# The second chunk's strided heads on TensorE in pairs, and a new order for the first chunk's heads

## The chip, the cores and the metric

One core of a Trainium2 chip runs the kernel. The metric is device time in microseconds (us), from one launch; the time given for a kernel is the median of several runs. The core's engines are named as the profile names them: PE (TensorE matmuls; PEld its weight loads), DVE (VectorE), ACT (ScalarE), POOL (GpSimd) and SP (SyncE, which here issues nearly all DMAs). Every engine carries out its own instructions strictly in the order in which they stand in its queue.

## What is computed

Attention with two kinds of masks, and then a two-layer network on its output:

```python
scores = scale * np.matmul(q, k.transpose(0, 1, 3, 2))        # 8 batches, 8 heads, 576 rows, 64 wide
mask_local = (rel >= 0) & (rel < 32)                           # heads 0 to 3
mask_strided = (rel >= 0) & (pos[None, :] % 32 == pos[:, None] % 32)   # heads 4 to 7
attn = softmax(where(mask, scores, -1e9))
x = (attn @ v) as 4608 x 512
h = np.maximum(x @ w_in, 0.0)                                  # 512 -> 2048
out = h * h @ w_out                                            # 2048 -> 512
```

All of it is in 32-bit floats. For the network the kernel splits each operand into a high and a low part and adds three products (high by high, low by high, high by low), so that one step of a layer costs three matmuls.

## The kernel before, in words

The 4608 tokens are worked off in 12 chunks of 384. For each chunk the attention of its rows comes first and fills four tiles of x: `xlh`, `xll` (local heads, high and low part) and `xsh`, `xsl` (strided heads). Then the network runs in 16 steps. `up` (L452) makes one 128-row slice of h from the four tiles: 12 matmuls of 384 columns (L462), the first 6 from the local tiles and the last 6 from the strided ones. ACT and DVE square it and split it (L470 to L476). `down` (L480) follows two steps later and adds 9 matmuls of 512 columns into three accumulators (L489). So PE has 21 matmuls in each of 16 x 12 steps, and the attention of chunk c+1 has to be finished while the network of chunk c runs.

Attention is done in three ways:

- **Pairs on PE** (`pe_pair`, L292): two heads at a time, from a tile `qk` that holds both heads' 64 rows. Five steps: load; scores on PE (L319) and row minima with the mask on DVE (L324); softmax (POOL subtracts the minima, L347, ACT takes the exponential, L348, DVE sums, L349, and takes the reciprocal, POOL multiplies, L353); transposes on PE (L359) and their copies from PSUM (L360); products with v on PE (L367 local, L378 strided), and the high and low part of x (ACT L382, DVE L383). In the first chunk both the local pairs (`first`) and the strided pairs (`late`) go this way, ahead of everything else. In the second chunk only the local pairs do (`local(c)`), and they have one PSUM bank, number 3, for all that PE writes: each write waits until the bank has been read out. The first chunk's local pairs use a shorter form, `single`, in which ACT subtracts the minimum, takes the exponential and sums in one instruction for each window (L345).
- **Strided heads on POOL and DVE** (`strided`, L386): products on POOL and sums on DVE, row by row: q by k (L412, L413), softmax (L418 to L425), attention by v (L434, L435), and transposes (L441). Chunks 2 to 12 of the 12 do their strided heads so.
- **Local heads one at a time on PE** (`pe_head`), from the third chunk on: among others the parts `kx` and `qx` (L217 to L220) and scores (L234).

While the first chunk's network runs, the weights are still arriving. `convert` (L147) turns each of 16 loads into a high and a low part, in two cuts of 512 columns: ACT scales the load (L154), makes `z` (L166) and the high part (L172), DVE joins two halves (L169), POOL makes the low part (L173). Two cuts belong to each step of the network (`WRATE`).

What sets the order: the main loop (L631) hands out the work by step. `SPREAD` (L43) says over how many steps of the running chunk the next chunk's local and strided work is handed out, here 11 and 8 in the first chunk. The program is then scheduled at build time, engine by engine, from the framework's own forecast of the time; the order in the finished queues is therefore not the order of the code. `zeros` (L583) are products of zeros on PE during the opening: 60, and then twice 30.

Of the kernel before, what the change touches and what calls it, by code (L numbers as in the profile page):

```python
# [17 lines left out]
HL = H // 2  # L18
# [24 lines left out]
SPREAD = ((11, 8), (13, 13))  # L43
# [43 lines left out]
def attn_moe(ctx: ExitStack, tc, qk_l, v_l, qk_d, v_d, qk_p, v_p, f_s, q_s, k_s, v_s, w_in, w_out, masks, eye, out):  # L87
# [59 lines left out]
    def convert():  # L147
# [9 lines left out]
        for k in range(NFT):  # L157
# [4 lines left out]
            for raw, at in cuts:  # L162
# [13 lines left out]

                if not at and k + 1 < NFT and k + 1 in raws:
                    with tc.issue_after(first_step.ins):
                        scale(k + 1)
# [112 lines left out]
    def pe_pair(c, pr, local, qk, vr, es, pt, banks, sm, single):  # L292
# [3 lines left out]
        if local:  # L296
            kw, wins, nv = KW, [at for _, _, at in windows(c)], P
            src, vsrc = qk_d[c, pr], v_d[c, pr]
            mk = [mask_sb[:QC, w % 2, :] for w in range(NW)]
        else:  # L300
            kw, wins, nv = QC, [QC * w for w in range(NW)], QC
            src, vsrc = qk_p[pr], v_p[pr]
            mk = [mask_sb[:QC, 3, :QC]] * NW
# [12 lines left out]
        e4 = [e[:QC, : NW * kw].rearrange("p (w k) -> p w k", k=kw) for e in es]  # L316
# [25 lines left out]
        for h in range(2):  # L342
            if single:
                for w in range(NW):
                    last["a"] = nc.scalar.activation(e4[h][:, w], e4[h][:, w], AF.Exp, bias=nm[:QC, h, w : w + 1], scale=-1.0, accum_out=ss[:QC, NW * h + w, :1])  # L345
# [6 lines left out]
        for h in range(2):  # L352
            last["g"] = nc.gpsimd.tensor_mul(e4[h], e4[h], rs[:QC, h].unsqueeze(2).broadcast_to([QC, NW, kw]))  # L353
        yield
        p4 = pt.rearrange("p (h w q) -> p h w q", h=2, w=NW)
        for h in range(2):
# [3 lines left out]
            last["a"] = nc.scalar.copy(pt[:kw, h * TC : (h + 1) * TC], t[:kw, :TC])  # L360
        yield
        x = x_tiles(c)
        if local:
# [4 lines left out]
            outs = [(o[:, :TC], [x["l", s][:, pr, :] for s in "hl"])]  # L368
        else:

            r0 = D * pr
            outs = []
            for a in range(2):
                o = s_ps[a]
# [5 lines left out]
                outs.append((o[r0 : r0 + D, :TC].rearrange("p (s r i) -> p s i r", s=2, i=SI), [by_i(x["s", s][:, a, :]) for s in "hl"]))  # L380
        for src, (xh, xl) in outs:
            last["a"] = nc.scalar.copy(xh, src)  # L382
            last["v"] = nc.vector.tensor_sub(xl, src, f32(xh))  # L383
# [156 lines left out]
    def local(c):  # L540
        heads = [pair_at(c, pr, True, pr, "3") for pr in range(2)]
        for h in (0, 0, 1, 0, 1, 0, 0, 1, 1, 1):
            next(heads[h])
            yield
# [58 lines left out]
    with tc.issue_after(last["p"].ins):  # L603
        zeros(0, NWARM // 2)
        for k in range(NEARLY, 8):
            fetch(k)
    next(late[0])
    with tc.issue_after(last["p"].ins):
        zeros(1, NWARM // 2)
    next(first[0])  # L610
    next(first[1])
    weights = behind({"a": last["a"]}, ungated)
    next(late[1])
    for i in range(2):
        next(first[0])
        next(first[1])
        next(late[0])
        next(late[1])
        if i:
            weights = behind({"a": last["a"]}, ungated)  # L620
        for _ in range(2):
            next(weights)
    next(late[0])
    next(late[1])
    for _ in range(2 * NEARLY - 4):
        next(weights)
# [4 lines left out]
    for s in range(NS + 2):  # L631
# [29 lines left out]
        if c + 1 < NCHUNK and s >= LATER:  # L661
            j0 = LATER if c == 0 else 0
            if j == j0:
                lo, st = local(c + 1) if c == 0 else iter(()), strided(c + 1)
                if c == 0:
                    lo, st = behind(heads_end, lo), behind(heads_end, st)
# [5 lines left out]
            while dl < fl * 10 and next(lo, "end") != "end":  # L672
# [14 lines left out]
def _layout(q, k, v, moe_w_in, moe_w_out):  # L687
# [22 lines left out]
    by_r = lambda t: rows(t[:, HL:], 0).reshape(HL, 2, SI, STR, D).transpose(0, 1, 3, 2, 4).reshape(HL, TC, D)  # L710
    a["qk_p"] = asc(np.concatenate([by_r(t).transpose(0, 2, 1) for t in (q, k)], axis=2)).reshape(2, P, 2 * TC)
    a["v_p"] = two(by_r(v).reshape(HL, NW, QC, D).transpose(0, 2, 1, 3).reshape(1, HL, QC, NW * D)).reshape(2, QC, 2 * NW * D)
# [45 lines left out]
```

## Time and profile before

| | us |
|---|---|
| median of 3 runs (883.71 to 884.16) | 883.96 |
| the profiled execution: its own time | 883.18 |
| its span, first to last instruction | 881.4 |
| first matmul of the network (L462) | 30.44 |
| first matmul of `down` (L489) | 39.17 |
| first matmul of the second chunk's network | 105.14 |

The 1.8 us between the profiled execution's own time and its span lie outside the instructions. The view of the timeline gives for each instruction its start and its duration; durations on one engine overlap a little, so starts, not durations, add up to the time. A bracket at the end of a row is idle time of the engine before it and what ended that. Matmuls with 32-bit operands appear as two records each.

### The profile page before, as it was taken

The page shows a single profiled execution, that of the slowest core. Times are in us where ns is not written, and L with a number is a line of the kernel's source. Part 1 is how long each engine was busy: PE and PEld are TensorE (multiplying, and loading weights), DVE is VectorE, ACT ScalarE, POOL GpSimd, SP SyncE. Part 2 cuts the span into 40 slices and gives each one's busy share as a digit, 9 for nine tenths or more (in the row PEclk, how much of TensorE's full clock was granted, in tenths as well). Part 3 has the DMA queues.
Part 4 walks back from the last instruction along what each step waited for, and adds up shares of the span by engine and source line. Part 5 has one row for each costly group of instructions (what it writes and reads, how often), then busy time and mean ns, then how long its engine had stood idle before and what let it go on. Part 6 is the DMA issues. An engine that isn't in the chain of part 4 may idle for free.

```text
span 881.4 us, 14862 instructions
## 1 busy us (share of the span) xinstructions
PE 868.5 (99%) x4744; PEld 789.6 (90%) x4744; DVE 635.5 (72%) x1892; ACT 572.6 (65%) x1510; POOL 676.8 (77%) x722
## 2 busy tenths in 40 slices
PE   8899999999999999999999999999999999999997
PEld 7788899999999999999999999999999989998996
DVE  4578687788777888878778778778787787883111
ACT  6798776676676666757657747657666665664332
POOL 4698878878978989898988978997898899782000
PEclk9999999999999999999999999999999999999999
DMA  9851631323123123104102302312131121000000
GB/s 356 355 195 63 184 121 42 103 84 113 32 66 112 37 89 103 44 30 127 44 13 80 115 14 74 104 31 74 31 102 57 30 71 61 7 1 10 28 1 36
DMA packets 26798, 71.41 MB, mean 81 GB/s; under 512 B 2976, under 2 KB 8736, under 8 KB 25184
## 3 DMA queue, kind: packets, MB, share of 16 engines
q1 hardware_dynamic: 26432, 70.14, 23.9%
q8 instruction: 37, 0.61, 0.3%
q10 hardware_dynamic: 288, 0.33, 0.1%
q14 instruction: 41, 0.34, 0.1%
HBM read 61.01 MB, written 9.44 MB: 80 GB/s over the span
## 4 chain that ended last, share of the span: by engine, by line
PE 95%; ACT 3%; DVE 1%; POOL 0%; issue 0%; DVEq 0%; POOLq 0%; ACTq 0%
PE h L462 44%; PE y L489 44%; PE s L234 2%; PE o L280 2%; ACT e L345 1%; PE w_ps L586 1%; ACT raw L154 1%; PE b L319 1%; DVE sc L419 0%; ACT z L166 0%; ACT w L172 0%; DVE raw L169 0%; ACT pt L360 0%; PE b L359 0%; DVE xsl L383 0%
## 5 line engine op out<-in xcount | busy, mean ns | idle before, releaser
L489 PE MATMUL y<-w,gh 128*128 128x512 f32 x1152 | 357.1, 391 | 0.8 <-ACT gh L475 0.8
L489 PEld LDWEIGHTS y<-w,gh 128*128 128x128 f32 x1152 | 212.5, 188 | 41.5 <-ACT gh L475 1.4
L462 PE MATMUL h<-xlh,w 128*128 128x384 f32 x768 | 229.6, 339 | 2.1 <-DVE xsl L383 1.6
L462 PE MATMUL h<-xsh,w 128*128 128x384 f32 x768 | 226.2, 335 | 0.0
L489 PE MATMUL y<-w,gl 128*128 128x512 f32 x576 | 224.0, 392 | 0.0
L434 POOL TENSOR_TENSOR pp<-vs,sc 128x448 f32<-128x448 f32 (+10 forms) x192 | 189.8, 1014 | 39.8 <-DVE qs L435 18.2
L412 POOL TENSOR_TENSOR pq<-ks,qs 128x512 f32<-128x512 f32 (+2 forms) x192 | 197.8, 1050 | 17.9 <-DVE sc L413 13.8
L476 DVE TENSOR_TENSOR gl<-h,gh 128x384 fp32r<-128x384 f32 x192 | 105.4, 550 | 84.2 <-ACT gh L475 82.9
L475 ACT CAST gh<-h 128x384 fp32r<-128x384 f32 x192 | 91.4, 477 | 103.0 <-PE y L489 100.0
L473 ACT ACTIVATE h<-h 128x384 f32<-128x384 f32 x176 | 83.0, 472 | 107.8 <-PE h L462 106.2
L413 DVE TENSOR_REDUCE sc<-pq 128x8 f32<-128x512 f32 (+4 forms) x228 | 119.6, 534 | 46.2 <-POOL pq L412 43.9
L462 PEld LDWEIGHTS h<-xlh,w 128*128 128x128 f32 x768 | 142.1, 188 | 5.6 <-DVE xsl L383 1.8
L462 PEld LDWEIGHTS h<-xsh,w 128*128 128x128 f32 x768 | 141.7, 188 | 0.3
L462 PE MATMUL h<-xll,w 128*128 128x384 f32 x384 | 129.3, 337 | 0.0
L435 DVE TENSOR_REDUCE qs<-pp 128x64 f32<-128x448 f32 (+11 forms) x192 | 106.7, 563 | 31.0 <-POOL pp L434 29.5
L489 PEld LDWEIGHTS y<-w,gl 128*128 128x128 f32 x576 | 108.1, 188 | 22.9
L462 PE MATMUL h<-xsl,w 128*128 128x384 f32 x384 | 128.5, 335 | 0.0
L474 ACT ACTIVATE h<-h 128x384 f32<-128x384 f32 x176 | 83.2, 473 | 3.6
L259 DVE STREAM_TRANSPOSE p_t<-e 32x128 f32<-32x128 f32 x240 | 72.3, 301 | 10.4 <-ACT e L248 6.0
L462 PEld LDWEIGHTS h<-xll,w 128*128 128x128 f32 x384 | 72.5, 189 | 2.2
L462 PEld LDWEIGHTS h<-xsl,w 128*128 128x128 f32 x384 | 72.2, 188 | 0.0
L243 ACT ACTIVATE e<-e,nm 96x128 f32<-96x128 f32 x160 | 62.5, 392 | 10.5 <-DVE nm L226 8.8
(97 smaller groups left out, 1077.2 us busy)
## 6 DMA issues: line engine op xcount, KB each, us to landing
qk<-qk_l SPq DMA_DIRECT2D x24, 400.0 KB, 3.2
y<-ysb SPq DMA_DIRECT2D x36, 256.0 KB, 3.7
raw<-w_in SPq DMA_DIRECT2D x7, 1024.0 KB, 11.2
qk<-qk_l SPq DMA_DIRECT2D x16, 416.0 KB, 3.3
vs<-v_s SPq DMA_DIRECT2D x10, 576.0 KB, 4.0
raw<-w_out SPq DMA_DIRECT2D x5, 1024.0 KB, 12.9
v<-v_l SPq DMA_DIRECT2D x40, 128.0 KB, 2.0
ks<-k_s SPq DMA_DIRECT2D x8, 576.0 KB, 3.8
```

What stands on the lines that cost most here:

```text
L243: nc.scalar.activation(e[:QC, cut(w)], e[:QC, cut(w)], AF.Exp, bias=nmax[:QC, w : w + 1], scale=-1.0, accum_out=ssum[:QC, w, :1])
L259: nc.vector.transpose(out=pt[STR * k : STR * (k + 1), :, STR * r : STR * (r + 1)], in_=e.rearrange("p (w k) -> p w k", k=KW)[STR * r : STR ...
L412: nc.gpsimd.tensor_mul(pv, kt[:, a : a + m, :], qt[:, i - i0 : i - i0 + 1, :].broadcast_to([P, m, D]))
L413: nc.vector.tensor_reduce(out=sc[:, i - i0, a : a + m], in_=pv, op=ALU.add, axis=AX.X)
L434: nc.gpsimd.tensor_mul(pv, vt[:, a : a + nd, :n], sc[:, il : il + 1, :n].broadcast_to([P, nd, n]))
L435: nc.vector.tensor_reduce(out=ot[:, il, a : a + nd], in_=pv, op=ALU.add, axis=AX.X)
L462: done = nc.tensor.matmul(ph[:, :TC], w[:, wsl], xx, start=n == 0, stop=n == 11)
L473: nc.scalar.activation(g, g, AF.Relu)
L474: nc.scalar.activation(g, g, AF.Square)
L475: last["gh"] = nc.scalar.copy(gh, g)
L476: nc.vector.tensor_sub(gl, g, f32(gh))
L489: done = nc.tensor.matmul(y_ps[c][t], g[:, sl], w[:, wsl], start=j == 0 and k == 0, stop=j == NFT - 1 and k == 2)
```

## The change

1. `local(c)` becomes `pairs(c)`: in the second chunk the strided pairs follow the local pairs, with the same buffers and the same single PSUM bank. `strided` is not run for that chunk; the host lays out `qk_p` and `v_p` for both chunks. The 20 steps are handed out over 12 network steps, the local pairs first.
2. Where a pair has one bank, its products with v take a bank for each half and are read out at once (`parts`), where before they were read out at the end.
3. In the first chunk the local pairs' exponentials are written to PSUM (`r4`) and multiplied from there by DVE instead of POOL, and the copies of the strided pairs' transposes (L360 before, L367 now) go from ACT to DVE.
4. The opening's steps come in a new order; the zeros are 60 and 20. The conversion of the first load's second cut is finished at once.

```diff
-SPREAD = ((11, 8), (13, 13))
+SPREAD = ((12, 8), (13, 13))
...
+                if k == 0 and at:
+                    split()
+                    split = None
...
+        r4 = [blocks(t) for t in s_ps] if single else e4
...
-                    last["a"] = nc.scalar.activation(e4[h][:, w], e4[h][:, w], AF.Exp, ...
+                    last["a"] = nc.scalar.activation(r4[h][:, w], e4[h][:, w], AF.Exp, ...
...
-            last["g"] = nc.gpsimd.tensor_mul(e4[h], e4[h], rs[:QC, h].unsqueeze(2).broadcast_to([QC, NW, kw]))
+            eng, key = (nc.vector, "v") if single else (nc.gpsimd, "g")
+            last[key] = eng.tensor_mul(e4[h], r4[h], rs[:QC, h].unsqueeze(2).broadcast_to([QC, NW, kw]))
...
-            last["a"] = nc.scalar.copy(pt[:kw, h * TC : (h + 1) * TC], t[:kw, :TC])
+            (nc.vector.tensor_copy if c == 0 and not local else nc.scalar.copy)(pt[:kw, h * TC : (h + 1) * TC], t[:kw, :TC])
...
+        def parts(src, dst):
+            last["a"] = nc.scalar.copy(dst[0], src)
+            last["v"] = nc.vector.tensor_sub(dst[1], src, f32(dst[0]))
...
-                o = s_ps[a]
+                o = s_ps[a] if s_ps else banks()
...
-    def local(c):
-        heads = [pair_at(c, pr, True, pr, "3") for pr in range(2)]
-        for h in (0, 0, 1, 0, 1, 0, 0, 1, 1, 1):
-            next(heads[h])
-            yield
+    def pairs(c):
+        for kind in (True, False):
+            heads = [pair_at(c, pr, kind, pr, "3") for pr in range(2)]
+            for h in (0, 0, 1, 0, 1, 0, 0, 1, 1, 1):
+                next(heads[h])
+                yield
...
-                lo, st = local(c + 1) if c == 0 else iter(()), strided(c + 1)
+                lo, st = (behind(heads_end, pairs(c + 1)), iter(())) if c == 0 else (iter(()), strided(c + 1))
...
-            while dl < fl * 10 and next(lo, "end") != "end":
+            while dl < fl * 20 and next(lo, "end") != "end":
```

What this does to the queues is seen in the finished order. Line numbers change: scores L319 become L325, transposes L359 L366, products with v L367 and L378 become L379 and L389, `up` L462 L470, `down` L489 L497, the low part of x L383 L373, POOL's subtraction and multiplication L347 and L353 become L353 and L360, its products L412 and L434 become L420 and L442.

First ACT's queue in the opening, where the last high parts of the strided heads' x (`xsh`) are made. Before:

```order
L382 CAST xlh_423<-b_1_1_218 128x384
L360 COPY pt_0_0_103<-b_0_0_280 96x384
L360 COPY w_1_0_104<-b_1_0_354 96x384
L382 CAST xsh_425<-b_0_0_279 64x384
L360 COPY w_1_0_104<-b_1_0_355 96x384
L166 ACTIVATE z_0_468<-raw_192 128x512
L172 CAST w_0_413<-raw_190 128x512
L154 ACTIVATE raw_194<-raw_194 128x1024
L382 CAST xsh_425<-b_0_0_280 64x384
L382 CAST xsh_425<-b_1_0_354 64x384
```

And now, at the same place of ACT's queue:

```order
L367 COPY pt_1_1_116<-b_1_1_218 128x384
L367 COPY pt_1_1_116<-b_1_1_219 128x384
L172 CAST w_0_372<-raw_190 128x512
L372 CAST xlh_384<-b_1_1_218 128x384
L372 CAST xsh_386<-b_0_0_248 64x384
L372 CAST xsh_386<-b_0_0_249 64x384
L372 CAST xsh_386<-b_1_0_313 64x384
L372 CAST xsh_386<-b_1_0_314 64x384
L166 ACTIVATE z_0_469<-raw_192 128x512
L154 ACTIVATE raw_194<-raw_194 128x1024
```

The four casts have moved ahead of the work on the second and third load, and the copies of the strided pairs' transposes have left the queue.

Next PE's queue at the border between the first and the second chunk's network; `b` is the pairs' PSUM bank, `h` the second chunk's first slices, `xlh` and `xll` its local x. Before, the last products of the pairs (`b`) lie among the first chunk's own steps, and the second chunk begins without any of them:

```order
L367 MATMUL b_1_1_1282<-pt_1_1_689,v_1_1_686 64x96 x8
L462 MATMUL h_14_1323<-xsh_425,w_7_1160 128x384 x2
...
L489 MATMUL y_2_614<-w_6_1218,gl_13_1307 128x512
L462 MATMUL h_0_1397<-xlh_901,w_0_413 128x384
L462 MATMUL h_0_1397<-xll_902,w_0_413 128x384
L462 MATMUL h_0_1397<-xlh_901,w_0_413 128x384 x2
```

Now the last local pair's products come after the second chunk's first six matmuls, and the whole of the strided pairs after that:

```order
L379 MATMUL b_1_1_969<-pt_1_1_648,v_1_1_645 64x96 x8
L470 MATMUL h_0_1392<-xlh_843,w_0_372 128x384
L325 MATMUL b_0_0_1039<-qk_0_0_1025 96x96 x4
L470 MATMUL h_0_1392<-xll_844,w_0_372 128x384
L325 MATMUL b_0_0_1048<-qk_0_0_1025 96x96 x4
L325 MATMUL b_1_0_1153<-qk_1_0_1030 96x96 x4
...
L366 MATMUL b_0_0_1210<-ident,e_0_0_1027 96x96 x4
L389 MATMUL b_0_0_1222<-pt_0_0_1029,v_0_0_1026 32x96 x8
...
L389 MATMUL b_1_0_1351<-pt_1_0_1034,v_1_0_1031 32x96 x8
L470 MATMUL h_0_1392<-xsl_846,w_0_372 128x384
...
L497 MATMUL y_0_571<-w_7_1199,gh_14_1309 128x512 x2
```

The strided pairs' scores, transposes and products stand in a row, with next to no matmul of the network between them, ahead of the second chunk's remaining matmuls and of the first chunk's last two `down` steps.

Last POOL's queue at the same place. `e` are the strided pairs' exponentials, `pp` and `pq` the products of `strided` for the third chunk, `kx` and `qx` parts of the third chunk's first local head:

```order
L353 TENSOR_TENSOR e_0_0_1028<-e_0_0_1028,nm_0_0_1037 96x384
L442 TENSOR_TENSOR pp_4_2_0_1626<-qkvs_4_1487,sc_4_1489 128x192
...
L353 TENSOR_TENSOR e_1_0_1032<-e_1_0_1032,nm_1_0_1151 96x384
...
L221 TENSOR_TENSOR kx_0_1335<-qk_0_1324,kx_0_1335 128x448
...
L360 TENSOR_TENSOR e_0_0_1027<-e_0_0_1027,rs_0_0_1038 96x384
...
L420 TENSOR_TENSOR pq_6_7_0_1751<-ks_6_1647,qs_6_1646 128x512
...
L360 TENSOR_TENSOR e_1_0_1032<-e_1_0_1032,rs_1_0_1152 96x384
...
L420 TENSOR_TENSOR pq_6_11_8_1844<-ks_6_1647,qs_6_1646 128x256
```

The second chunk's strided softmax shares POOL with the third chunk's strided heads, and the two alternate. DVE's queue interleaves them in the same way: between the four low parts of x (L373) stand the sums (L421) of the `pq` products.

53 lines of the change are left out of this document (25 added, 28 removed).

## Prediction

> **What bounds the kernel now.** I read the page first, then the timeline of PE for every stretch in which it stands idle, then the chain of waits for the opening.
>
> ```profile
> PE 868.5 (99%) x4744; PEld 789.6 (90%) x4744; DVE 635.5 (72%) x1892; ACT 572.6 (65%) x1510; POOL 676.8 (77%) x722
> ```
>
> PE is busy for all but 13 us. From the timeline of PE, the start of the first chunk's network, its first `down`, the one later gap, and the border to the second chunk:
>
> ```profile
> 30.44 0.69 PE L462 MATMUL h<-xlh,w 128*128 128x384 f32 x1 [1.61 <-DVE xsl L383]
> ...
> 39.17 1.66 PE L489 MATMUL y<-w,gh 128*128 128x512 f32 x6 [0.79 <-ACT gh L475]
> ...
> 89.56 0.44 PE L462 MATMUL h<-xlh,w 128*128 128x384 f32 x1 [0.48 <-DVE gl L476]
> ...
> 105.14 0.33 PE L462 MATMUL h<-xlh,w 128*128 128x384 f32 x1
> ```
>
> After 39.17 PE waits for another engine once, for 0.48. So work that leaves POOL and DVE is worth at most that 0.48, matmuls that are added to PE cost their full time, and time is to be had only ahead of 39.17. The stages of the opening, with the granted clock in the third column from the end:
>
> ```profile
> 25.00:30.00 5.00, 3.56 (x67) 2.85 (x66) 1.40 (x3) 4.13 (x8) 1.51 (x2) 1.00 1.01 422
> 30.00:35.00 5.00, 4.56 (x18) 4.56 (x19) 2.80 (x5) 4.69 (x9) 2.64 (x2) 0.66 1.01 405
> ```
>
> After a stretch with PE busy for 3.56 of 5 us, the clock falls for the network's first matmuls (0.66 on average), so the 36 `up` matmuls up to 39.17 take 8.7 us instead of the 6.3 that three times this row gives:
>
> ```profile
> 41.51 2.10 PE h L462 x12
> ```
>
> **The opening.** The network begins when the strided heads' low parts of x are made, and ACT's casts for them stand at the end of its queue. The chain of waits has the opening's prices on ACT:
>
> ```profile
> 8.76 6.27 ACT e L345 x32
> 15.03 1.08 ACT raw L154
> 16.11 0.41 ACT e L348
> 16.52 0.36 ACT pt L360
> ...
> 18.08 0.53 ACT z L166
> ...
> 19.72 0.36 ACT xlh L382
> ...
> 21.39 0.56 ACT w L172
> ...
> 30.42 0.87 DVE xsl L383 x2
> ```
>
> In the new order ACT has ahead of the last cast: the 16 window exponentials (6.27), 4 strided ones (1.7), 4 copies (1.5), 2 scalings (2.2), 2 `z` (1.1), 2 high parts (1.1) and 6 casts (2.2), together 16.1 us; from 8.76 that ends at 24.9. DVE now becomes the longer one:
>
> ```profile
> 0.00:30.40 30.40, 23.53 (x312) 20.48 (x312) 13.71 (x83) 20.75 (x60) 14.19 (x24) 1.00 0.95 372
> ```
>
> To its 13.7 us come four multiplications of 512 columns from PSUM (about 0.7 each, an estimate from the 0.55 that DVE takes for 384, below) and four copies (about 0.5), and one joining of weights comes later (0.6): 18 us. DVE starts just ahead of ACT's 8.76, so it ends at 26.5. The first matmul needs the bank that the second of the four low parts frees, some 0.7 before the end: 25.8. The 36 `up` matmuls take 6.3, the low clock about 1.8: the first `down` at 34.0 instead of 39.17, a gain of 5.2. Bounds: 2.6, if DVE keeps half of its old idle time, and 8, if ACT's sum is the limit and the clock stays up. The 40 zeros that go were hidden behind waits for the softmax; what they may cost is the clock of the opening's small matmuls, which is in the lower bound. That ACT now waits for the first two slices before it goes on with the weights belongs to the second rival.
>
> The removed POOL and DVE work of `strided` gives the 0.48, no more.
>
> **The added matmuls, if they were spread out.** Scores of one strided head, eight records one head after the other; transposes; products with v:
>
> ```profile
> 15.31 0.92 PE L319 MATMUL b<-qk 64*96 64x96 f32 x8
> ...
> 24.48 0.54 PE L359 MATMUL b<-ident,w 96*96 96x96 f32 x4 [1.34 <-POOL w L353]
> ...
> 27.32 1.51 PE L378 MATMUL b<-w,v 96*32 96x96 f32 x30 [0.28 <-ACT w L360]
> ```
>
> Without the last record's drain (a quarter of a microsecond) that is 0.68 a head for scores, 0.33 a head for transposes and 0.7 for each half of a pair's products: 4 x 0.68 + 4 x 0.33 + 4 x 0.7 = 6.8 us. Both heads of a pair alternately, as the first chunk issues them, cost less, here in the wider local form:
>
> ```profile
> 7.21 1.99 PE L319 MATMUL b<-qk 64*96 64x128 f32 x32
> ```
>
> That is 0.06 a record, against 1.04 us for eight (0.13) for one head at a time:
>
> ```profile
> 54.35 1.04 PE b L319 x8
> ```
>
> The second chunk's pairs don't do what the change's words say: in PE's queue they go one head at a time, so I take 0.68. The Trainium skill, TensorEngine Tiling (Array Packing), Tiling Modes, says that different tiles can load weights and multiply in parallel; by that rule, issued alternately, the scores would cost half and the sum would be 1.4 lower. The trace agrees with it in the first chunk.
>
> **Where they stand.** The queue decides more than the 6.8. At the border PE comes to the strided pairs with all other matmuls behind them: six of the second chunk's first 24 `up` matmuls are done, 18 and `down` 14 and 15 come later. So PE waits out the pairs' whole softmax, one bank at a time. POOL's share of that chain, from the groups by line and shape:
>
> ```profile
> L353 POOL TENSOR_TENSOR e<-e,rs 96x384 f32<-96x384 f32 x2 | 1.6, 822 | 0.0
> L347 POOL TENSOR_TENSOR e<-e,nm 96x384 f32<-96x384 f32 x2 | 1.6, 820 | 0.0
> L434 POOL TENSOR_TENSOR pp<-qkvs,sc 128x384 f32<-128x384 f32 x4 | 3.9, 964 | 0.0
> L434 POOL TENSOR_TENSOR pp<-qkvs,sc 128x320 f32<-128x320 f32 x4 | 3.5, 884 | 0.1
> L434 POOL TENSOR_TENSOR pp<-qkvs,sc 128x256 f32<-128x256 f32 x4 | 3.3, 816 | 0.0
> L434 POOL TENSOR_TENSOR pp<-qkvs,sc 128x192 f32<-128x192 f32 x4 | 2.2, 552 | 0.0
> L218 POOL TENSOR_TENSOR kx<-qk,kx 128x448 fp32r<-128x448 f32 x6 | 6.9, 1158 | 5.3 <-ACT kx L217 4.3 <-POOL xll L288 1.0
> L220 POOL TENSOR_TENSOR qx<-qk,qx 64x384 fp32r<-64x384 f32 x5 | 5.1, 1013 | 0.4
> L412 POOL TENSOR_TENSOR pq<-ks,qs 128x512 f32<-128x512 f32 x8 | 10.3, 1294 | 0.6 <-DVE qkvs L435 0.4 <-DVE sc L413 0.2
> L412 POOL TENSOR_TENSOR pq<-ks,qs 128x448 f32<-128x448 f32 x2 | 2.3, 1152 | 0.1
> L446 POOL TENSOR_TENSOR xsl<-qkvs,xsh 128x384 fp32r<-128x384 f32 x4 | 4.1, 1015 | 0.0
> L255 POOL TENSOR_TENSOR vx<-v,vx 128x256 fp32r<-128x256 f32 x5 | 3.7, 743 | 0.1
> ```
>
> And the hops on DVE and ACT:
>
> ```profile
> L324 DVE CUSTOM_DVE_ANT_0 e<-b,mask_sb 96x96 f32<-96x96 f32 x8 | 1.5, 243 | 0.0
> L349 DVE TENSOR_REDUCE sums<-e 96x4 f32<-96x384 f32 x2 | 1.1, 545 | 1.1 <-ACT e L348 1.1
> L383 DVE TENSOR_TENSOR xsl<-b,xsh 64x384 fp32r<-64x384 f32 x4 | 2.1, 553 | 3.8 <-ACT xsh L382 3.8
> L360 ACT COPY pt<-b 96x384 f32<-96x384 f32 x2 | 0.9, 475 | 0.0
> L382 ACT CAST xsh<-b 64x384 fp32r<-64x384 f32 x4 | 1.8, 472 | 0.3 <-PE b L378 0.3
> ```
>
> I count from the end of the last local pair's products. Cast and low part 1.0; scores 0.9; minima 1.0 (4 x 0.243); the second head the same 1.9: at 4.8 POOL can subtract its minima. From there POOL always has work, and its queue up to the last `pq` that DVE sums ahead of the last low part of x is: 3 subtractions (2.5), `pp` of 192, 256, 320 and 384 columns (3.2), `kx` and `qx` (2.2), 4 multiplications (3.3), `pq` of 448 and five of 512 (7.6), `xsl` and `vx` (1.8), and four short `pq` and a memset (about 2.3, an estimate from the sizes). Together 22.9. Then the sum of that `pq` (0.4), the low part (0.55), the last four `up` matmuls (0.9). End at 29.5. DVE sums each `pq` ahead of the low part that frees the bank, so the products with v and the second pair's transposes wait for POOL too; ACT's exponentials of the second pair stand behind a cast of `kx`, whose load cannot start before the strided scores free its buffer, but that ends ahead of POOL.
>
> The 18 `up` matmuls in this stretch would have cost 3.1 anyway. The stretch costs 26.4, the added matmuls included.
>
> **The clock.** With PE mostly idle for that long, the row at 30 us says that the clock falls; then the eight transposes and products after it take 4 us more, of which half lies behind POOL, and the next matmuls some 0.5: 2.5 in all. Both ends stay: 0 and 5.7 (4 and half of one 3.4 us stretch at half clock). The Trainium skill, TensorE: Matmul & The Clock Gate, Part 1, wants a whole idle window of about 3.4 us for the fall; by that rule alone a busier stretch stays at full speed and the sum is 2.5 lower. The trace shows the fall after a stretch that was mostly busy, so I go by the trace.
>
> **Sum**, against the profiled execution's own 883.2 (0.8 under the median): 883.2 - 5.2 - 0.5 + 26.4 + 2.5 = 906.4 us.
>
> **Rivals.** Two of them go by this row, a stretch of the first chunk's network (busy time of PE, PEld, DVE, ACT, POOL):
>
> ```profile
> 39.20:60.00 20.80, 20.80 (x107) 18.56 (x107) 16.88 (x46) 20.34 (x37) 18.04 (x19) 1.00 0.38 129
> ```
>
> *The queue behind the softmax is thinner.* If the third chunk's POOL work has been done before PE gets there, only the chain remains: 4.8 as above, the softmax's subtraction, exponential, sum, reciprocal and multiplication (0.8 + 0.5 + 0.5 + 0.4 + 0.8), for each pair two transposes with their copies (2.0) and two products with v, casts and low parts (3.9), and the last 0.9: 20.5 us, less 3.1. Then 883.2 - 5.7 + 17.4 = 895. For it: POOL was busy for 18.0 of 20.8 us, so it has some time in hand. Against it: POOL's new queue has that work after the strided subtractions, and a queue doesn't run ahead. 10%.
>
> *ACT becomes the bound of the first chunk.* Its work in a network step is two cuts and a slice, and it was busy for 20.3 of the 20.8 us. PE now starts 5 us earlier and asks for the weights earlier. If ACT follows only at its own pace, PE waits up to 5 us around the sixth slice: 911. For it: that share. Against it: ACT's opening ends as much earlier as PE's. 10%.
>
> *Faster.* The opening gains more than the border costs. It decides in this direction if the stretch at the border takes under 8.8 us, the opening's 5.2, the 0.5 and the 3.1: PE would have to find other matmuls while the pairs wait. With all of the wait filled and the opening's upper bound it is 883.2 - 8 - 0.5 + 6.8 = 881.5. For it: nothing but the short opening. Against it: a queue can't pass a waiting matmul, and the opening can't pay for the border by itself: the first load is scaled at 15.03, which with `z` and the high part is 2.2 on ACT, and joining and the low part on DVE and POOL are about as much again, so the network can hardly start before 20, which with the 2.4 of the slow first matmuls and the 0.5 is 13.3, under the 17.4 of the shortest chain. 3%, and 1% for no change.
>
> **How the numbers follow.** The forecast has 76%. The range runs from 894 (the thinner queue) to 914 (the forecast with the slow clock's upper end, or ACT's wait on top of it with a short opening). About 0.2% (1.8 us) is what a measurement of this kernel tells from no change; faster 0.03, same 0.01, slower 0.96.
>
> **What would show it.** The first `up` near 26 and the first `down` near 34. Then a stretch of 28 to 32 us beginning near 101, in which PE is busy for about a third, with its idle time ended by POOL's multiplication, ACT's copies and DVE's low parts; POOL without a break in it; and the clock below 1 toward its end. Outside of it the same pace as before. It is wrong if PE shows no gap over 3 us at the border, or if the network starts no earlier than 30.

## The result, and the profile after

| | before | after |
|---|---|---|
| median of 4 runs each, one chip, us | 883.84 (883.00 to 884.16) | 911.92 (909.73 to 915.61) |
| ratio, with its 95% interval | | 1.0324 (1.0299 to 1.0348) |
| profiled execution: own time, span | 883.18, 881.4 | 912.86, 911.1 |
| mean granted clock | 0.997 | 0.975 |

The change makes the kernel 28 us slower. The forecast, 906.4 with 894 to 914, had the sign and the cause, but of its terms the opening's gain came out far too large, the border's price too small. Here and below, ratios compare the means of the runs, and leave out the single executions of 1436 to 2218 us that before, `opening_warm` and `opening_hold` had once each.

From the page of the changed kernel, busy time of the engines, and the granted clock in 40 slices of 22.8 us:

```profile
PE 885.7 (97%) x4816; PEld 802.6 (88%) x4816; DVE 636.6 (70%) x1904; ACT 574.4 (63%) x1514; POOL 662.8 (73%) x698
...
PEclk8899859999999999999999999999999999999999
```

POOL and PE's idle time show what was exchanged: POOL has 14 us less to do than before, and PE, which was idle for 13 us, is idle for 25. The clock is low twice, in the first two slices (the opening) and in the fifth and sixth (the border). Everything behind the sixth is as before.

From PE's timeline in the changed kernel (start, duration, and in brackets the idle time ahead and what ended it): the first `up` (L470) and first `down` (L497), and the second chunk's first `up`:

```profile
30.36 0.45 PE L470 MATMUL h<-xlh,w 128*128 128x384 f32 x1
...
38.61 0.98 PE L497 MATMUL y<-w,gh 128*128 128x512 f32 x3 [1.04 <-ACT gh L483]
...
102.50 0.34 PE L470 MATMUL h<-xlh,w 128*128 128x384 f32 x1
```

30.36 stands against 30.44, 38.61 against 39.17, 102.50 against 105.14: the opening, which was to gain 5.2, gains 0.56, and the first chunk's network another 2.08. Of that 0.48 is the wait for DVE which is gone, and 0.8 are the last local pair's products, which have moved behind 102.50.

Then the border, from the last local products (L379) to the first matmul behind the second chunk's 24th `up`:

```profile
103.65 0.88 PE L379 MATMUL b<-pt,v 128*64 128x96 f32 x16
...
107.09 0.92 PE L325 MATMUL b<-qk 64*96 64x96 f32 x8 [1.36 <-DVE xll L373]
...
111.88 1.59 PE L325 MATMUL b<-qk 64*96 64x96 f32 x8 [0.89 <-DVE nm L330]
114.36 1.59 PE L325 MATMUL b<-qk 64*96 64x96 f32 x8 [0.89 <-DVE nm L330]
120.11 0.87 PE L366 MATMUL b<-ident,e 96*96 96x96 f32 x4 [4.16 <-POOL e L360]
121.64 0.84 PE L366 MATMUL b<-ident,e 96*96 96x96 f32 x4 [0.66 <-POOL e L353]
123.05 1.50 PE L389 MATMUL b<-pt,v 96*32 96x96 f32 x16 [0.56 <-ACT pt L367]
125.70 1.50 PE L389 MATMUL b<-pt,v 96*32 96x96 f32 x16 [1.16 <-DVE xsl L373]
128.44 0.85 PE L366 MATMUL b<-ident,e 96*96 96x96 f32 x4 [1.25 <-DVE xsl L373]
130.00 0.84 PE L366 MATMUL b<-ident,e 96*96 96x96 f32 x4 [0.71 <-ACT pt L367]
131.41 1.50 PE L389 MATMUL b<-pt,v 96*32 96x96 f32 x16 [0.56 <-ACT pt L367]
133.48 1.01 PE L470 MATMUL h<-xsh,w 128*128 128x384 f32 x2 [0.57 <-ACT xsh L372]
...
139.03 0.63 PE L237 MATMUL s<-kx,qx 128*96 128x256 f32 x4
```

From 102.50 to 139.03 are 36.53 us; before, the same 24 matmuls went from 105.14 to 109.62, in 4.48. (The network's matmuls appear as one record each, those of the pairs as two.) The border costs 32.05. With -0.56 and -2.08 that is +29.4 of the +29.68 between the two profiled executions.

The same stretch in two parts, up to the first transposes and from there on (length; busy time of PE, PEld, DVE, ACT and POOL; clock):

```profile
104.45:120.11 15.66, 7.79 (x40) 6.14 (x38) 10.75 (x56) 3.25 (x7) 11.66 (x17) 0.62 0.37 126
120.11:139.03 18.92, 13.45 (x92) 10.49 (x93) 9.62 (x25) 5.52 (x13) 14.05 (x18) 0.51 0.10 31
```

In the first part PE ends up waiting for POOL (4.16 us ahead of 120.11); the clock is already low in it, from 108.08 on, and the later scores take 1.59 instead of 0.92. In the second nearly every wait is for ACT's or DVE's next step on the one bank, and PE's own steps take long: 0.85 for four transposes instead of the 0.54 of before's opening, 1.50 for sixteen products. That suggested three prices, POOL's queue, the clock, and the chain itself, and the experiments separate them in part.

### The profile page after: what moved, and what is told of

Its sections match the earlier page's. It is cut to its first block, busy times and chain, and to the rows that moved or that the text cites. A ratio compares the mean times of both kernels' runs of the same rounds, so it can differ in the third digit from the quotient of the medians.

```text
span 911.1 us, 15008 instructions
## 1 busy us (share of the span) xinstructions
PE 885.7 (97%) x4816; PEld 802.6 (88%) x4816; DVE 636.6 (70%) x1904; ACT 574.4 (63%) x1514; POOL 662.8 (73%) x698
## 4 chain that ended last, share of the span: by engine, by line
PE 86%; ACT 2%; POOL 1%; DMA 1%; DVE 1%; issue 0%; DVEq 0%; POOLq 0%; ACTq 0%
PE h L470 41%; PE y L497 40%; PE s L237 2%; PE o L283 2%; PE b L389 1%; PE b L325 1%; POOL w L173 1%; DMA qkvs<-f_s 0%; DMA raw<-w_out 0%; ACT w L172 0%; ACT z L166 0%; ACT raw L154 0%; POOL pq L420 0%; PE b L366 0%; DVE e L330 0%
## 5 line engine op out<-in xcount | busy, mean ns | idle before, releaser
L497 PE MATMUL y<-w,gh 128*128 128x512 f32 x1152 | 356.7, 391 | 1.0 <-ACT gh L483 1.0
L497 PEld LDWEIGHTS y<-w,gh 128*128 128x128 f32 x1152 | 212.4, 188 | 41.3 <-ACT gh L483 1.4
L470 PE MATMUL h<-xlh,w 128*128 128x384 f32 x768 | 229.3, 339 | 0.6 <-ACT xlh L372 0.6
L470 PE MATMUL h<-xsh,w 128*128 128x384 f32 x768 | 227.2, 337 | 0.6 <-ACT xsh L372 0.6
L497 PE MATMUL y<-w,gl 128*128 128x512 f32 x576 | 224.6, 392 | 0.0
L420 POOL TENSOR_TENSOR pq<-ks,qs 128x512 f32<-128x512 f32 (+2 forms) x192 | 197.7, 1048 | 25.5 <-DVE sc L421 17.2
L442 POOL TENSOR_TENSOR pp<-vs,sc 128x448 f32<-128x448 f32 (+10 forms) x192 | 189.8, 1013 | 31.1 <-DVE qs L443 15.4
L421 DVE TENSOR_REDUCE sc<-pq 128x8 f32<-128x512 f32 (+3 forms) x216 | 114.9, 543 | 51.1 <-POOL pq L420 48.6
L470 PEld LDWEIGHTS h<-xlh,w 128*128 128x128 f32 x768 | 141.5, 188 | 4.0 <-ACT xlh L372 0.8
L470 PEld LDWEIGHTS h<-xsh,w 128*128 128x128 f32 x768 | 142.3, 189 | 1.6 <-ACT xsh L372 0.9
L470 PE MATMUL h<-xll,w 128*128 128x384 f32 x384 | 129.4, 337 | 0.0
L470 PE MATMUL h<-xsl,w 128*128 128x384 f32 x384 | 129.2, 336 | 0.0
L497 PEld LDWEIGHTS y<-w,gl 128*128 128x128 f32 x576 | 108.0, 188 | 23.0
L470 PEld LDWEIGHTS h<-xll,w 128*128 128x128 f32 x384 | 72.3, 188 | 2.4
L470 PEld LDWEIGHTS h<-xsl,w 128*128 128x128 f32 x384 | 72.6, 189 | 0.3 <-issue 0.3
## 6 DMA issues: line engine op xcount, KB each, us to landing
raw<-w_out SPq DMA_DIRECT2D x5, 1024.0 KB, 12.5
```

What stands on the lines that cost most here:

```text
L420: nc.gpsimd.tensor_mul(pv, kt[:, a : a + m, :], qt[:, i - i0 : i - i0 + 1, :].broadcast_to([P, m, D]))
L421: nc.vector.tensor_reduce(out=sc[:, i - i0, a : a + m], in_=pv, op=ALU.add, axis=AX.X)
L442: nc.gpsimd.tensor_mul(pv, vt[:, a : a + nd, :n], sc[:, il : il + 1, :n].broadcast_to([P, nd, n]))
L470: done = nc.tensor.matmul(ph[:, :TC], w[:, wsl], xx, start=n == 0, stop=n == 11)
L497: done = nc.tensor.matmul(y_ps[c][t], g[:, sl], w[:, wsl], start=j == 0 and k == 0, stop=j == NFT - 1 and k == 2)
```

## The experiments

The theory: the whole loss is the strided pairs' chain at the border, in front of which PE's in-order queue stands still; within it the third chunk's work on POOL and the low clock each have a price. The opening's gain was lost to the low clock. The rivals stand in the expectations.

### One half of the change alone

`opening_only` keeps the new opening and gives the second chunk's strided heads back to POOL and DVE:

```diff
-        for kind in (True, False):
+        for kind in (True,):
...
-                lo, st = (behind(heads_end, pairs(c + 1)), iter(())) if ...
+                lo, st = (behind(heads_end, pairs(c + 1)), behind(heads_end, strided(c + 1))) if ...
```

> The changed opening, with the second chunk's strided heads back on POOL and DVE as before. If the pairs at the border of the first two chunks make the whole loss, this kernel has no gap there and ends within 1.5 us of before (about 883.3: the first down 0.56 us earlier, as in the changed kernel's trace, and the rest at before's pace). If instead the new opening costs something that lasts through the first chunk (the weights' parts come in another order, the maxima move from POOL to DVE), it is 2 us or more slower than before. The first up is expected at 30.4, with the granted clock at 0.5 from about 16 to 30, as in the changed kernel.

`border_only` is the kernel before with points 1 and 2 of the change and its old opening.

> Before's opening, unchanged, with the second chunk's strided heads on TensorE as in the changed kernel. If the border alone makes the loss: 911 to 914, with the clump of scores, transposes and products between the two chunks 33 to 36 us long and the clock at half in it. If half of the loss came of how the new opening leaves the queues of ACT, DVE and POOL, it is under 900.

Measured: 881.90 and 913.36 against 883.82 before; ratios 0.9994 (0.9977 to 1.0010) and 1.0335 (1.0315 to 1.0355). The border alone makes the whole loss. The opening alone is not to be told from before.

But its profile wasn't what I expected. From PE's timeline of `opening_only`:

```profile
26.82 0.45 PE L470 MATMUL h<-xlh,w 128*128 128x384 f32 x1
...
34.88 0.96 PE L497 MATMUL y<-w,gh 128*128 128x512 f32 x3 [1.02 <-ACT gh L483]
...
106.00 0.45 PE L470 MATMUL h<-xsl,w 128*128 128x384 f32 x1 [1.53 <-POOL xsl L454]
...
107.87 0.63 PE L237 MATMUL s<-kx,qx 128*96 128x256 f32 x4
```

With the same opening instructions the first `down` comes at 34.88, 4.3 earlier than before and not far from the forecast's 34.0. At the border 1.75 of it is left (107.87 against 109.62): PE now waits for POOL's low part of the strided x, which it did not before, and once for DVE's `gl`, 1.38 us at 43.09 (before, 0.48 at 89.56). The difference to the changed kernel's 38.61 is the clock, but for 0.45 us by which `opening_only` was ahead at its first transposes (13.68 against 14.13). PE's busy time and clock in the clock's own 3.41 us steps, first of the changed kernel, then of `opening_only`:

```profile
12.51:15.92 3.41, 1.04 (x8) 1.00 1.01 416
15.92:19.34 3.42, 1.61 (x15) 0.50 1.02 419
19.34:22.75 3.41, 3.41 (x25) 0.50 1.01 420
22.75:26.16 3.41, 3.41 (x26) 0.50 1.01 423
26.16:29.58 3.42, 3.42 (x50) 0.50 1.01 419
```

```profile
11.56:14.98 3.42, 1.15 (x10) 1.00 1.00 412
14.98:18.39 3.41, 1.11 (x8) 0.50 1.01 416
18.39:21.80 3.41, 3.41 (x28) 0.50 1.01 423
21.80:25.22 3.42, 3.42 (x57) 1.00 1.01 422
```

Both fall to half after a window with PE busy for a third. The one stays there for four windows, the other for two. The runs of `opening_only` divide accordingly: eight at 881.2 to 883.2 with a mean clock of 0.994 to 0.996, four at 885.1 to 888.1 with 0.988 to 0.992.

### More zeros for the opening's clock

`opening_warm` (on `opening_only`) and `after_warm` (on the changed kernel) have 60 zeros where these have 20:

```diff
-    zeros(1, NWARM // 3)
+    zeros(1, NWARM)
```

> The same kernel with 60 products of zeros instead of 20 between the opening's scores and transposes, which keep TensorE busy for about 2.5 us longer. Theory one, the clock ate the opening's gain: the granted clock stays at 1.0 past 16, the transposes and products of 16 to 30 take half as long, first up at 27 or earlier, the kernel 2.5 to 4 us faster than before (880 to 881.5). Rival, ACT and DVE set the opening's end whatever the clock does: the first up stays within 1 us of 30.4 and the time within 1 us of the kernel with 20 zeros.

> The whole change, with 60 zeros instead of 20 in the opening. If opening and border add up, this gains as much over the changed kernel as the 60 zeros gain without the border: 2 to 4 us, 908 to 910. Rival, the earlier network only meets the border's stall earlier and waits longer there, since that stall ends with POOL and DVE work that does not move: 911 to 913.

Measured: 887.20, ratio 1.0038 (1.0025 to 1.0050), and 915.82, ratio 1.0362 (1.0343 to 1.0382). Both are worse than without, by 5.3 and 3.9 us, opposite to the theory; neither rival named it either. PE's timeline of `opening_warm` shows how:

```profile
27.21 0.45 PE L470 MATMUL h<-xlh,w 128*128 128x384 f32 x1 [0.68 <-DVE xsl L373]
...
29.53 1.51 PE L389 MATMUL b<-w,v 96*32 96x96 f32 x30 [0.36 <-DVE w L367]
...
39.20 0.50 PE L497 MATMUL y<-w,gh 128*128 128x512 f32 x1 [1.06 <-ACT gh L483]
```

The zeros hold up the second strided pair's scores, the scheduler then puts its products last, between the first `up` matmuls, and the first `down` comes at 39.20. The clock fell in it all the same, only later; it was low from 18.8 to 25.6. So the kernel shows that this pair has no time to spare, and nothing of what a clock at 1.0 would be worth. That the same edit costs 5.3 and 3.9 with and without the pairs at the border fits opening and border adding up; it can't show it closer than that.

Three more kernels change the opening. `opening_fill` puts 30 and 40 zeros into the waits themselves, into a bank of the second strided pair. `opening_gate` has 50 zeros and holds the transposes behind the last scores. `opening_later` is `opening_only` with the third chunk's strided work behind the low part that PE waited for at 106.00; two memsets and the start of that work also come one step later.

```diff
+    fill(30)
+    with tc.issue_after(last["z"].ins):
+        next(first[0])
+    with tc.issue_after(last["t"].ins):
+        fill(40)
```

> The changed opening without the border's pairs, as in opening_only, with 70 more products of zeros in the very waits of TensorE: 30 behind the last scores, 40 behind the first transposes, held there so that the order of the rest stays (opening_warm's 40 zeros changed that order, and the second strided pair came last there). If the waits from 12 to 18 are what lets the clock fall, it stays at 1.0 until the network, first up at 25.5 to 27 in every run, and the time is 880 to 882 with no runs at 885 to 888 as opening_only has. Rival: the fall is not set by these waits, the runs go on to differ by 4 to 5 us, median within 1 us of opening_only.

> opening_only with 50 zeros instead of 20, and the first transposes behind the last scores, so that the second strided pair is not late as it was in opening_warm. If the waits of TensorE near 12 decide the opening's clock, it falls later or not at all, first up at 26 to 27 in every run, no runs at 885 to 888, median 880.5 to 882. Rival: it falls in the waits from 15 to 18 just the same, or the later scores of the second strided pair cost what the clock gains: 883 or more.

```diff
-                    st = behind(weights_end, st)
+                    st = behind({**weights_end, "g": ends}, st)
```

> opening_only with the third chunk's strided heads behind the last low part of the second chunk's on POOL, and the two memsets of the transposes' buffers one step later. In opening_only TensorE waits 1.53 us at 106.0 for that low part, which stood behind 1.7 us of such work. If that is where the opening's gain of 4.3 us at the first down goes, this is 1 to 1.5 us faster than opening_only: 880.5 in runs where the opening's clock comes back early. Rival: ups ahead of it wait for something else by then (ACT's casts, DVE's sums), and it is within 0.4 us of opening_only.

Measured: `opening_fill` 883.83, ratio 0.9998 (0.9988 to 1.0008); `opening_gate` 889.72, 1.0053 (1.0035 to 1.0071); `opening_later` 884.44, 0.9991 (0.9976 to 1.0006). In `opening_fill` the zeros share a bank with scores that DVE has yet to read, and wait for it themselves:

```profile
15.25 3.03 PE L600 MATMUL b<-p_t 128*128 128x128 bf16 x30 [3.27 <-DVE nm L330]
```

After that the clock is low for one window only, and its eleven runs lie at 883.3 to 885.4 with clocks of 0.996 to 0.998, no longer in two groups; but the wait has eaten the gain: the first `up` is at 28.54, and the median is neither the 880 to 882 that was expected nor within 1 us of `opening_only`. In `opening_gate` the clock falls all the same, from 17.5 to 27.7, as its rival had it, and the first `up` comes at 31.82; the clock gave nothing there. In `opening_later` the wait at the border shrinks to 0.71; its runs lie at 880.5 to 881.5 (clock 0.996, five) and 884.2 to 885.1 (0.992, seven). It is 0.6 us better than `opening_only` where the clock is 0.995 or 0.996, less than the 1 to 1.5 expected, and 1.5 better where it is 0.992 (three runs of `opening_only`). By its median it is no better than before.

`opening_hold`, the last, adds zeros to `opening_later` that should wait for nothing: 32 ahead of the last scores, 40 behind the first transposes in the first strided pair's bank.

> opening_later with zeros that wait for nothing late: 32 instead of 20 ahead of the last scores, and 40 behind the first transposes, in the first strided pair's bank (its maxima are done by then, so the 3.27 us wait of opening_fill should not come), the first products held behind them. In every record so far the clock fell in the 3.41 us window behind one in which TensorE was busy for 0.57 of the time or less, and held behind 0.63 or more. Theory one, that share decides: the windows from 11 to 18 are 0.6 busy or more, the clock stays at 1.0 up to the network, first up at 25.5 to 27 in every run, 879.5 to 881.5 and no runs at 884 to 885. Rival: the second strided pair, whose scores come 0.75 us later and whose products now stand last, sets the first up at 28 or later, and the time is 882 or more with the clock at 1.0.

Measured: 882.84, ratio 0.9994 (0.9982 to 1.0006). The clock stays up through the opening as intended, but the first `up` is at 28.05, since the second strided pair is last again, and at the border PE waits for POOL; the rival holds.

```profile
107.49 0.44 PE L471 MATMUL h<-xsl,w 128*128 128x384 f32 x1 [1.75 <-POOL xsl L455]
```

No version of the opening that ran is measurably better than the kernel before: what it gains at the start, PE gives back to POOL's strided heads at the border and to DVE ahead of it, or in the opening to the second strided pair.

### What the border's length is made of

`pool_later` holds the third chunk's strided heads back until the last strided pair's low part:

```diff
-                    st = behind(weights_end, st)
+                    st = behind({**weights_end, "x": last["x"]}, st)
```

> The changed kernel, with the third chunk's strided heads held back until the last strided pair's low part (all but two of their first multiplications, and DVE's sums of them, leave the border). Theory one, the queue: those multiplications stand ahead of the pairs' softmax on POOL and DVE. The border's first scores come about 1.4 us earlier (DVE's low part no longer waits behind the third chunk's sums), POOL's first pair of 0.8 us multiplications 2 to 3.5 us earlier than at 119.24, the second pair's up to 1.6 us: the stretch from 104.4 to 139.0 is 4 to 6 us shorter, the time 906 to 908. Rival, the chain: one bank and the order scores, maxima, next scores, then transposes, copy, products, low part hold the length whatever POOL has besides, so the stretch stays within 1.5 us of 34.6 and the time within 1.5 us of 911.9. A loss of over 2 us would mean that the third chunk's strided heads then come too late for their own border.

Measured: 909.24, ratio 1.0272 (1.0250 to 1.0294), between what the two theories expected. The two parts of the stretch, beside 15.66 and 18.92:

```profile
104.94:115.93 10.99, 5.42 (x40) 4.07 (x39) 5.58 (x38) 2.92 (x6) 5.46 (x7) 0.83 0.49 170
115.93:135.03 19.10, 13.63 (x92) 10.64 (x93) 4.32 (x11) 5.01 (x11) 5.69 (x8) 0.50 0.11 30
```

The stretch is 4.5 us shorter, within the 4 to 6 of the first theory, and all of that lies in the first part. In the second POOL is busy for 5.7 us instead of 14.1 and the length is the same: there POOL's queue does not set the pace. PE's scores in `pool_later` show that not all of the 4.5 is the queue:

```profile
106.19 0.92 PE L325 MATMUL b<-qk 64*96 64x96 f32 x8
...
109.80 0.92 PE L325 MATMUL b<-qk 64*96 64x96 f32 x8 [0.89 <-DVE nm L330]
111.60 1.11 PE L325 MATMUL b<-qk 64*96 64x96 f32 x8 [0.89 <-DVE nm L330]
```

The first scores come 1.4 us earlier after the local products, and the first transposes follow the last scores 1.4 us sooner: that is the queue. But 1.86 lie between the first and the fourth scores (5.41 us instead of 7.27), where the waits for DVE are the same 0.89 and the scores take 0.92 instead of 1.59: here the clock fell at 112.2, in the changed kernel at 108.1. So the total agreed with the first theory, and its parts did not; the second pair, for which it had up to 1.6, gained nothing. How the first part lost its time to the queue is seen on POOL in the changed kernel:

```profile
103.26 3.74 POOL L420 TENSOR_TENSOR pq<-qkvs 128x64 f32<-128x64 f32 x6 [1.44 <-DMA qkvs<-f_s]
...
116.06 1.13 POOL L221 TENSOR_TENSOR kx<-qk,kx 128x448 fp32r<-128x448 f32 x1
117.27 0.99 POOL L223 TENSOR_TENSOR qx<-qk,qx 64x384 fp32r<-64x384 f32 x1
118.33 0.94 POOL L442 TENSOR_TENSOR pp<-qkvs,sc 128x384 f32<-128x384 f32 x1
119.24 1.61 POOL L360 TENSOR_TENSOR e<-e,rs 96x384 f32<-96x384 f32 x2
```

The third chunk's first products start when their load lands, at 103.26; DVE's sums of them stand ahead of its low part `xll`, for which the first scores wait (1.36 us at 107.09). And four operations of the third chunk stand ahead of the pair's multiplication at 119.24.

`border_warm` and `border_both` put dummy products, whose results nothing reads, into TensorE's waits, the first in the changed kernel, the second on top of `pool_later`:

```diff
                 for w in range(NW):
                     scores(h, w, s)
+                if not local:
+                    spin(s, 24)
```

> The changed kernel with dummy products into unused columns of the strided pairs' bank at the border (24 behind each head's scores, 12 behind each head's transposes and ahead of each half of the outputs; nothing reads them), so that TensorE has work in its waits. Theory one, the clock: the granted clock stays at 1.0 or falls later, the transposes (0.87 us for four), products (1.50 for sixteen) and ups after 120 take some 60% of it, and the stretch is 5 to 6 us shorter: about 906. Rival: the pieces of the chain are latency of ACT, DVE and POOL and not TensorE's time, so that the clock's return gains under 1.5 us, or the dummies cost what they gain: 910.5 to 913.

> Both edits: the third chunk's strided heads held back and the dummy products at the border. If the queue and the clock are two separate parts of the stretch, the gains add: 9 to 12 us below the changed kernel, 900 to 903, with 23 to 26 us left from the local heads' last products to the last up; still 15 us or more slower than before, which is the price of the chain itself. If they are one (whichever is taken away, the other holds the length), it gains no more than the better of the two alone.

Measured: 923.98, ratio 1.0435 (1.0413 to 1.0458), and 918.75, 1.0392 (1.0371 to 1.0414). Neither says what the clock costs: the dummies write to the pairs' bank, and so became links of the chain. In `border_warm` scores wait for them:

```profile
116.89 0.89 PE L330 MATMUL b<-qk 64*96 64x96 f32 x8 [1.01 <-PE b L298]
```

In `pool_later_warm` the dummies have a bank of their own and their numbers are chosen to fit the waits. The second chunk's strided pairs are also handed out later, behind all ten steps of the local ones.

```diff
+    def spin(n, ins):
+        some = ident[:, : P // 2].bitcast(BF16)
+        if not idle:
+            idle[0] = psum(0, "idle")
+        with tc.issue_after(ins.ins):
+            for _ in range(n):
+                nc.tensor.matmul(idle[0][:, :P], some, some, start=True, stop=True)
...
-            while dl < fl * 20 and next(lo, "end") != "end":
+            while dl < (10 if c == 0 else fl * 20) and next(lo, "end") != "end":
```

> pool_later with dummy products in TensorE's waits at the border, this time into a bank of their own (the next up's, free until then), so that no step of the pairs waits for them; 14 to 45 behind scores, 10 behind transposes, 18 behind the first three output halves. In pool_later the stretch from the local heads' last product to the last up takes 30.1 us, with the clock at half from 112.2. If the clock is a cost of its own there: it stays at 1.0 or falls for a shorter time, and the halved pieces of pool_later's second half (four groups of transposes, 0.85 to 0.53 us each; four halves of outputs, 1.50 to 0.87; ten ups, 3.4 to 1.7) give 4 to 6 us: stretch 24 to 26, time 903 to 905. If the chain's latency is what counts, it gains under 1.5 us. What stays at full clock, 24 us or so against the 3.1 of TensorE's own ups, is the price of the chain of softmax and low parts through one bank.

Measured: 905.91, ratio 1.0256 (1.0233 to 1.0279). The two parts:

```profile
101.16:115.93 14.77, 11.68 (x128) 10.29 (x126) 6.45 (x41) 2.57 (x5) 4.87 (x6) 0.88 0.31 98
115.93:129.68 13.75, 13.31 (x189) 11.28 (x187) 2.63 (x6) 4.25 (x10) 2.86 (x4) 1.00 0.05 12
```

The second part, now at full clock, takes 13.75 instead of 19.10: the clock's price there is 5.35 us, in the expected 4 to 6. The whole stretch, 28.5, and the time missed the expected 24 to 26 and 903 to 905, because the first part is longer than `pool_later`'s 10.99. That has reasons of this kernel's own: one load comes late, and the dummies behind the last scores, part of them at half clock, hold up the first transposes until 115.93.

```profile
109.14 0.89 PE L335 MATMUL b<-qk 64*96 64x96 f32 x8 [2.44 <-DMA qk<-qk_p]
...
112.39 3.70 PE L303 MATMUL idle<-ident 128*128 128x128 bf16 x45
```

So the stretch of 34.6 us can be put together, as an estimate from parts of different kernels, one profiled execution each: 11.0 (`pool_later`) and 13.75 (`pool_later_warm`) for the chain, 24.7 together; some 2.6 for the third chunk's work in the queues; and some 7.2 for the clock, 5.35 in the second part and 1.86 in the first. No run had the whole chain at full clock with empty queues, and the 11.0 is not the bare chain: in `pool_later` the third chunk's `kx` and `qx` still stand ahead of the pair's multiplication on POOL (112.78 to 115.05). Queues and clock together are no more than a third. Without them the change still loses: the 18 `up` matmuls in the stretch are worth 3.1.

## Why the prediction was right or wrong

**Where the pairs stand: right.** PE reached the strided pairs with everything else behind them, and nothing else of the change cost anything that `opening_only` could show.

**The opening, -5.2: wrong, -0.56.** The step that failed is the one on the clock: the 40 zeros that went were put down as hidden, with their price in the lower bound of 2.6, and so the end was worked out from ACT's and DVE's sums alone. Without them PE is busy for 1.04 of 3.41 us from 12.5 on, the clock falls, and from 19 to 30 PE itself is the longest of the three engines, without an idle moment; ACT waits 3.05 us for it ahead of 26.52. With zeros in the waits (`opening_hold`) the clock held up to the network. Where it came back after two windows, the first `down` was at 34.88, within 0.9 of what was worked out; but PE was the last engine there too, so ACT's and DVE's sums were not tried by themselves. The bound was too tight. Nor were the 2.4 us beyond 6.3 for before's 36 `up` matmuls all the clock's: the row at 39.17 has a wait of 0.79 for ACT in it, and the changed kernel, at full clock from 30.36, has one of 1.04 at the same place. The gain would not have lasted anyway: in `opening_only`, without the pairs at the border, only 1.75 of 4.3 reached the end of the second chunk's first 24 `up` matmuls.

**The strided work that left POOL and DVE, -0.5: too small, -2.08**, of which 0.8 only moved behind the border. Another 0.48 is the wait for DVE that the forecast had. The remaining 0.8 I can't place.

**The border, 26.4: too small in a way that the forecast's own picture explains only in part.** I walked POOL's queue to the end and let it pace the whole stretch: 29.5, with the clock 32. POOL did pace the end of the first part, but not the second, where the chain through one bank at half clock was longer than POOL's queue; `pool_later` took 8 us of POOL's work out of the second part and its length didn't change. Two sizes failed. The clock took some 7.2 by the estimate above, not 2.5, and went past its bound of 5.7: I had put half of the small matmuls' extra time behind POOL, which was not there to hide it, and had not counted the scores. And the third chunk's load, which wasn't in the walk at all, set the start of POOL's and DVE's work ahead of `xll` (1.36 us). Without the clock some 27.4 of the 34.6 are left, less than the walk's 29.5: a queue taken too long and a clock taken too cheap partly made up for each other, and that the border's sum came as near as 3 us is in part luck. "POOL without a break" was wrong too: it had breaks of 1.98, 1.26 and 0.41 up to 114.45.

**The rival of a thinner queue** had the chain at 20.5; the estimate from `pool_later` and `pool_later_warm` has 24.7. **ACT as the bound of the first chunk** did not come in the changed kernel, whose network started no earlier. Where it did start earlier, in `opening_only`, PE waited in that chunk once, 1.38 us for DVE. **The trace's word on the clock**, that it falls though PE is never idle for a whole window, held: at the border it fell after a window with PE busy for 1.61 of 3.41 us.

**The signs.** One of the two signs of being wrong came: the network starts at 30.36, no earlier than 30. The other did not: at the border PE has a gap of 4.16. The stretch is 34.6 us long instead of 28 to 32, PE is busy for 21.2 of it and not for a third, and the clock is low from 108.1, not only toward the end.

In sum: -2.6 where -5.7 was forecast, and +32.05 where 28.9 was. Two misses of 3 us in the same direction, and the range, which reached 914, took both.

## What to carry to other kernels

When a change puts a dependent chain into the queue of the engine that bounds the kernel, count the chain from end to end with everything behind it in that queue; work spared on other engines pays only what their waits showed. Walk every queue that the chain passes, but check at each step which of them is really last: a queue that is long on paper may end before the chain does. Time bought at the start must be followed to the next meeting point with a slower engine before it is booked.

## What the runs showed of the hardware

The granted clock changes in steps of 3.41 us whose phase to the kernel differs from run to run: the opening's stretch at half clock is two steps long in `opening_only` (14.98 to 21.80) and four in the changed kernel (15.92 to 29.58). It falls though PE was not idle for the whole step before. PE's busy share in that step does not decide it alone, though it looks so in two places of `opening_hold` (length, PE busy, clock):

```profile
13.06:16.48 3.42, 1.96 (x28) 1.00 1.01 419
16.48:19.89 3.41, 2.91 (x46) 1.00 1.01 416
...
33.54:36.96 3.42, 1.92 (x9) 1.00 1.03 408
36.96:40.37 3.41, 3.41 (x9) 0.50 1.05 391
```

After 1.96 of 3.42 us (0.57) it stayed, after 1.92 (0.56) it fell, and the expectation of that run took a share of about 0.6 for the edge. But in `border_only` it fell after 2.06 of 3.41 (0.60):

```profile
22.63:26.04 3.41, 2.06 (x34) 1.00 1.00 413
26.04:29.45 3.41, 3.31 (x38) 0.50 1.01 423
```

And in `opening_hold` it stayed at 1.0 after the step from 105.23 to 108.64, with PE busy for 1.66 of 3.41 (0.49; the wait of 1.75 shown above lies in it). What else counts stays open.

None of these steps was idle as a whole. The Trainium skill, TensorE: Matmul & The Clock Gate, Part 1, says that the window of about 3.4 us runs freely, which these runs bear out, and that the clock is low after at least one idle window; here windows a third to six tenths busy were enough, and the measurement decides. It also says that the clock is back after at least one busy window. `opening_only` needed one (a full window at half clock, 18.39 to 21.80), the changed kernel three, from 19.34 to 29.58. What decides between one and three stays open; in `opening_later` the medians of the two groups of runs, 881.12 and 884.77, lie 3.65 us apart.
